# Attention, routed experts and a bilinear layer in one kernel: one branch for the general path, other banks for the seven products, gate weights padded to 128 columns

## The chip, the core and the metric

The kernel runs on one core of a Trainium2 chip. The core has TensorE (PE) for matmuls, with a loader for weights (PEld), VectorE (DVE), ScalarE (ACT), GpSimd (POOL) and a sync engine (SP) that issues most transfers. Each engine takes its own instructions in order, and they wait for each other through semaphores. Matmuls write into PSUM, which the kernel divides into eight banks of 128 x 512 words. The metric is device microseconds of one execution; lower is better.

## What is computed

The reference has three steps, one after the other, all in float32:

```python
# windowed attention: B, H, S, D = 4, 8, 576, 64; window 128, a bias by distance
attn = softmax(where(mask, scale * q @ k.T + bias, -1e9)) @ v
x = attn.transpose(0, 2, 1, 3).reshape(2304, 512)
# routed experts: 8 of them, 512 -> 1024 -> 512; each token goes to its best one
logits = x @ w_gate + modality_bias[modality_id]
x = gate_w[:, None] * (relu(x @ w1[e]) @ w2[e])      # e = argmax(logits)
# bilinear layer: 512 -> 1024, a product, 1024 -> 1024, 1024 -> 512
out = ((x @ m_w1) * (x @ m_w2)) @ m_w3 @ m_wout
```

## The kernel before

Nearly every product is made of three matmuls: each factor is split into a high part (an ACT copy, names ending in h) and the rest (a DVE subtraction, names ending in l), by `split` (lines 249 and 251), and high x high, high x low and low x high are summed (`mm3`, lines 266 to 268). The work goes through four stages.

*Attention* (about 0 to 264 us) runs over 40 units (a chunk of tokens and four heads; here a chunk has 128 tokens, or 64 at the end of a sequence): scores `S`, softmax, transposes of the probabilities, and `av`, the product with v, which has 64 columns. When a tile of 128 tokens is done, `gate_logits` (line 465) transposes it (`xtp`) and makes the logits `lg` in four products with the gate weights `wg`, which have 8 columns, one per expert (line 478). The trace shows each of these products as two rows. There are 18 such tiles in five groups, and after each group `route` finds the experts and ranks. In the same stage PE makes the product of `m_w3` and `m_wout` (`pw`, `w_step`), by a list of steps written out by hand (`W_STEPS`).

*The bridge* (264 to 303) makes the table of blocks and gathers the tokens; the rest of `pw` is done under it.

*The experts* (303 to 540) take five static blocks of 480 tokens (`NB_STATIC`), with tiles `ph` and `py`. Another number of blocks can be needed for other tokens; that is the general path, below. Under this stage DVE and ACT make sums of `m_w1` and `m_w2` for the next one.

*The bilinear layer* (540 to 818) goes over three groups g of 768 tokens. Each has eight steps f (`ab_step`, line 1183) and six tiles j (`out_step`, line 1234). A step f makes two products of 2 x 2 blocks with seven block products instead of eight: seven times six matmuls of 128 x 384 (line 1196), summed in four banks `x`, `y`, `z`, `v` with the tags S, V, P and G. S and P have two banks each, V and G one. The first halves of `x` and `v` are read (a copy `c1` by ACT, sums `c22`, `c12`, `c21` by DVE, line 1205) and then a second product is added into the same bank. The weights of a step are loaded (`load_wt`) and split (`split_wt`: two `wth` on ACT, two `wtl` on DVE) one step ahead, and the sums of the next group's x (`x2_sum`, seven splits `x2h`/`x2l`) come behind the first tile j. A tile j makes `po` in 24 matmuls of 128 x 512 with `ab` (split by `ab_split` in halves `abh`, `abl`) and `Whl`, the split product of W3 and Wout; its banks have the tag A, two of them. ACT scales it (`o`, line 1245) and POOL scatters it (line 1246). The `wh` splits of that product are made in the eight steps of group 0.

*The general path* stands at the end (lines 1312 to 1335), behind `If`s on the number of blocks `nb`. `rest(b)` is called for each static block and for the next one, and the bilinear layer comes a second time. With the inputs here `nb` is 5, and none of the seven `If`s is taken; each engine jumps over each part (lines 1315 and 1333).

What sets the order on an engine is the order of the program, unless a scheduler finds an instruction ready earlier: it follows the order in which the program is written, with priorities (`tc.high_priority`), and `tc.issue_after(x)` keeps what stands in it behind x on its engine. A tile of a pool with a tag waits until the tile that had its buffer is released.

Of the kernel before, what the change touches and what calls it, by code (L numbers as in the profile page):

```python
# [33 lines left out]
EARLY = 2  # L34
W_STEPS = [0, 0, 0, 0, 0, 0, 0, 0, 0, 0, 1, 1, 1, 2, 1, 2, 1, 1, 1, 2, 0, 1, 0, 2, 1, 1, 1, 0, 0, 3, 2, 1, 0, 1, 1, 0, 0, 2, 1, 1, 1, 2, 2, 1, 3, 0]
# [8 lines left out]
def kernel(  # L44
# [67 lines left out]
    wg = const.tile([P, ND, E], F32, tag="wg", name="wg")  # L112
# [94 lines left out]
    def build_constants2():  # L207
# [3 lines left out]
        nc.sync.dma_start(out=wg, in_=w_gate.rearrange("(c p) e -> p c e", p=P))  # L211
# [479 lines left out]
    def w3_transposes(i):  # L691
        x = st_w.pop(("x", i))
        h = w_p.tile([P, 4, P], F32R, tag="w3h", name=f"w3h_{i}", bufs=3)
        l = w_p.tile([P, 4, P], F32R, tag="w3l", name=f"w3l_{i}", bufs=3)
        tp = pst("A", [P, 4, P], f"w3tp_{i}")
        for j in range(4):
            nc.tensor.transpose(tp[:, j, :], x[:, j * P : (j + 1) * P], ident)
        split(h, l, tp)
        st_w["T", i] = (h, l)
# [6 lines left out]
    def w_step(k):  # L706
# [8 lines left out]
        if g == NG - 1:  # L715
            last["ev", fc] = nc.scalar.copy(wraw[:, fc, :], pw)
# [73 lines left out]

    def chunk_done(b, c):
# [5 lines left out]
        if j == groups[g][1] - 1:  # L797
            todo.append(lambda: route(g, *groups[g]))
# [232 lines left out]
    def run_blocks(b0, b1, extra, after=None):  # L1031
        g0, g1 = b0 * NS, b1 * NS
        for g in range(g0, min(g0 + SA, g1)):
            if after is None:
                split_w(g)
            else:
                with tc.issue_after(after):
                    split_w(g)
# [23 lines left out]
    for n in range(k_in, n_w):  # L1062
# [7 lines left out]
        w_step(n)  # L1070
    wstk.close()
# [91 lines left out]
    def split_wt(g, f):  # L1163
        w = wt[g, f] = []
        for k in range(2):
            h, l = (
                f_p.tile([P, 7, P], F32R, tag=f"w{x}", name=f"wt{x}_{g}_{f}_{k}", bufs=4)
                for x in "hl"
            )
            split(h, l, wt.pop(("raw", g, f, k)))  # L1170
            w.append((h, l))

    def bilinear(first):
# [9 lines left out]
        def ab_step(g, f):  # L1183
# [4 lines left out]
                for tag, n in (("S", 2), ("V", 1), ("P", 2), ("G", 1))  # L1188
# [15 lines left out]
            def add(out, in0, in1, op=ALU.add):  # L1204
                nc.vector.tensor_tensor(out=out, in0=in0, in1=in1, op=op)  # L1205
# [3 lines left out]
            c1, u, c22, c12, c21 = tmp("c1"), tmp("u"), tmp("c22"), tmp("c12"), tmp("c21")  # L1209
            prod(x, A11, B11, True)  # L1210
# [6 lines left out]
            add(c22, z, c22)  # L1217
            prod(x, A12, B21, False)
# [3 lines left out]
            prod(v, A22, T4, False)  # L1222
            add(c21, v, u)
            add(ab[g][:, f, TS:], c21, c22, ALU.mult)

        def ab_split(g, j, i):
# [4 lines left out]
            split(ah, al, ab[g][:, i * NMC // 2 : (i + 1) * NMC // 2, cs])  # L1231
            ab[g, j, i] = (ah, al)
# [21 lines left out]
        g2 = {}  # L1254
        if not first:
# [4 lines left out]
            split_wt(0, 0)  # L1260
            load_wt(0, 1)
        for g in range(NG2):
# [36 lines left out]
    jobs.setdefault(g_end - 1, []).append(lambda: split_wt(0, 0))  # L1299
    jobs.setdefault(g_end - 1, []).append(lambda: load_wt(0, 1))  # L1300
    jobs.setdefault(g_end - 1, []).append(load_nb)
    run_blocks(0, NB_STATIC, jobs, last["ev", NMC - 2].ins)
# [9 lines left out]
    def rest(b):  # L1312
        if b == NB_MAX:
            return
        with tc.If(nb > (b if b > NB_STATIC else NB_STATIC)):
            first_loads(b, b + 1)
            run_blocks(b, b + 1, {})
            if b + 1 > NB_STATIC:
                rest(b + 1)

    with tc.tile_pool(name="xr", bufs=2) as x_p, tc.tile_pool(name="fr", bufs=2) as f2_p:

        def h_tiles(b, m):
            return tuple(
                f2_p.tile([P, BLK], F32R, tag=f"h{x}", name=f"h{x}r_{b}_{m}", bufs=HB) for x in "hl"
            )
# [8 lines left out]
    x2stk.close()  # L1335
# [38 lines left out]
```

## Time and profile before

| | |
|---|---|
| median of 3 runs | 851.11 us (849.89 to 856.74) |
| the profiled execution | 848.0 us, of which the span of the trace is 846.3 |
| mean granted clock of PE | 0.943 of full speed |
| PE busy | 791.3 us (93%) in 4405 instructions |
| weight loads | 693.3 us (82%) |
| DVE, ACT, POOL busy | 519.8 (61%), 352.1 (42%), 73.7 (9%) |

The span is what the trace covers; 1.7 us of the profiled execution lie around it. A busy share near 100% means that PE always had a matmul under way, not that it streamed at its peak. [...]

### The profile page before, as it was taken

The page shows a single profiled execution, that of the slowest core. Times are in us where ns is not written, and L with a number is a line of the kernel's source. Part 1 is how long each engine was busy: PE and PEld are TensorE (multiplying, and loading weights), DVE is VectorE, ACT ScalarE, POOL GpSimd, SP SyncE. Part 2 cuts the span into 40 slices and gives each one's busy share as a digit, 9 for nine tenths or more (in the row PEclk, how much of TensorE's full clock was granted, in tenths as well). Part 3 has the DMA queues.
Part 4 walks back from the last instruction along what each step waited for, and adds up shares of the span by engine and source line. Part 5 has one row for each costly group of instructions (what it writes and reads, how often), then busy time and mean ns, then how long its engine had stood idle before and what let it go on. Part 6 is the DMA issues. An engine that isn't in the chain of part 4 may idle for free. (4 is left out here: it accounts for less than half of the span.)

```text
span 846.3 us, 12536 instructions
## 1 busy us (share of the span) xinstructions
PE 791.3 (93%) x4405; PEld 693.3 (82%) x4405; DVE 519.8 (61%) x1273; ACT 352.1 (42%) x755; POOL 73.7 (9%) x102
## 2 busy tenths in 40 slices
PE   8999999999999899999999999998999979999960
PEld 6897878898997678887888889997889968899750
DVE  4758596657567539796885644768446693476310
ACT  5846465765752423333345534334323252322220
POOL 4000200110102312020010000000100001100110
PEclk9959889999979999999999999997999989999985
DMA  8985464345212846969587425424223421240010
GB/s 153 366 241 142 113 169 124 63 117 125 77 38 77 221 141 204 311 187 329 168 287 236 167 67 182 151 95 131 100 81 100 127 92 38 81 131 3 25 57 9
DMA packets 126443, 116.88 MB, mean 138 GB/s; under 512 B 69597, under 2 KB 100701, under 8 KB 126350
## 3 DMA queue, kind: packets, MB, share of 16 engines
q1 hardware_dynamic: 119853, 101.16, 41.4%
q0 software_dynamic: 3616, 9.66, 3.6%
q10 hardware_dynamic: 2880, 4.92, 1.6%
q8 instruction: 47, 0.77, 0.4%
q14 instruction: 47, 0.38, 0.2%
HBM read 87.85 MB, written 27.68 MB: 137 GB/s over the span
## 5 line engine op out<-in xcount | busy, mean ns | idle before, releaser
L383 ACT ACTIVATE p<-p,mn 128x256 f32<-128x256 f32 (+2 forms) x144 | 67.8, 473 | 26.6 <-DVE mn L378 26.4
L251 DVE TENSOR_TENSOR fwl<-fw,fwh 128x1024 fp32r<-128x1024 f32 x40 | 48.7, 1223 | 48.4 <-ACT fwh L249 44.4
L249 ACT ACTIVATE fwh<-fw 128x1024 fp32r<-128x1024 f32 x40 | 42.1, 1060 | 73.9 <-PE ph L267 57.9
L266 PE MATMUL ph<-xbh,fwh 128*128 128x480 f32 x160 | 61.9, 388 | 3.1 <-DVE Whl L956 2.4
L249 ACT ACTIVATE wth<-wt 128x896 fp32r<-128x896 f32 x48 | 43.8, 948 | 48.9 <-PE pP L1196 32.7
L426 PE MATMUL av<-vr,pT 128*128 128x64 f32 x448 | 63.1, 286 | 0.0
L426 PEld LDWEIGHTS av<-vr,pT 128*128 128x128 f32 x448 | 60.9, 208 | 1.7 <-DVE w_wo L652 0.2
L267 PE MATMUL ph<-xbl,fwh 128*128 128x480 f32 x160 | 61.6, 385 | 0.0
L378 DVE CUSTOM_DVE_ANT_0 p<-S,bias 128x256 f32<-128x256 f32 (+1 forms) x128 | 43.4, 386 | 29.5 <-PE S L352 29.3
L267 PE MATMUL py<-Whl,fwh 128*128 128x480 f32 x160 | 61.2, 383 | 0.0
L268 PE MATMUL ph<-xbh,fwl 128*128 128x480 f32 x160 | 61.2, 382 | 0.0
L266 PE MATMUL po<-Whl,abh 128*128 128x512 f32 x144 | 58.2, 404 | 1.9 <-ACT abh L249 1.9
L251 DVE TENSOR_TENSOR wtl<-wt,wth 128x896 fp32r<-128x896 f32 x48 | 52.0, 1083 | 12.1 <-ACT wth L249 9.2
L268 PE MATMUL py<-Whl,fwl 128*128 128x480 f32 x160 | 59.1, 380 | 0.0
L267 PE MATMUL po<-Whl,abh 128*128 128x512 f32 x144 | 57.9, 402 | 0.0
L266 PE MATMUL py<-Whl,fwh 128*128 128x480 f32 x160 | 56.9, 380 | 0.0
L268 PE MATMUL po<-Whl,abl 128*128 128x512 f32 x144 | 56.4, 395 | 0.0
L251 DVE TENSOR_TENSOR abl<-ab,abh 128x512 fp32r<-128x512 f32 x36 | 24.6, 689 | 48.9 <-ACT abh L249 48.9
L249 ACT ACTIVATE abh<-ab 128x512 fp32r<-128x512 f32 x36 | 22.4, 630 | 67.3 <-PE po L267 56.0
L1205 DVE TENSOR_TENSOR c<-pG,u 128x384 f32<-128x384 f32 x48 | 26.6, 554 | 37.7 <-PE pG L1196 37.3
L404 PE MATMUL PT<-ident,p 128*128 128x128 f32 x224 | 42.9, 310 | 0.0
L1246 POOL DMA_INDIRECT out_dram<-o,sid x18 | 17.8, 990 | 283.0 <-ACT o L1245 278.7
(236 smaller groups left out, 2010.8 us busy)
## 6 DMA issues: line engine op xcount, KB each, us to landing
wt<-wT SPq DMA_DIRECT2D x48, 448.0 KB
fw<-in_moe_w_dram SPq DMA_DIRECT2D x40, 512.0 KB
raw_w<-in_moe_w_dram SPq DMA_DIRECT2D x16, 512.0 KB
raw_m<-in_moe_w_dram SPq DMA_DIRECT2D x32, 256.0 KB
wT<-ms SPq DMA_DIRECT2D x16, 448.0 KB
yT<-zf SPq DMA_DIRECT2D x20, 256.0 KB
yT<-y ACTq DMA_DIRECT2D x20, 240.0 KB
x<-yT SPq DMA_DIRECT2D x12, 384.0 KB
```

The costliest lines, as they stand in the source:

```text
L249: last["a"] = nc.scalar.activation(out=hi, in_=src, func=AF.Copy, scale=scale)
L251: last["v"] = nc.vector.tensor_tensor(out=lo, in0=src, in1=f32(hi), op=ALU.subtract)
L266: nc.tensor.matmul(dst, lhsT=lh, rhs=rh, start=start, stop=False)
L267: nc.tensor.matmul(dst, lhsT=lh, rhs=rl, start=False, stop=False)
L268: return nc.tensor.matmul(dst, lhsT=ll, rhs=rh, start=False, stop=stop)
L378: nc.vector.tensor_tensor_reduce(out=p[:, j, t, :nk], in0=s[j][:, t, :nk], in1=bi, scale=1.0, scalar=BIG, op0=ALU.add, op1=ALU.min, accum_ ...
L383: nc.scalar.activation(out=p[:, j, t, :nk], in_=p[:, j, t, :nk], func=AF.Exp, scale=-1.0, bias=m1, accum_out=sm[:, col : col + 1],)
L404: nc.tensor.transpose(pt[:, t, kb, :], p[:, j, t, kb * P : (kb + 1) * P], ident)
L426: nc.tensor.matmul(av[:, h, :], lhsT=pT[:, j, t, kb, :], rhs=raw["v", b, cc][:, h, :], start=(i == 0), stop=(i == len(kbs) - 1),)
L1205: nc.vector.tensor_tensor(out=out, in0=in0, in1=in1, op=op)
L1246: sc = nc.gpsimd.indirect_dma_start(out=out, out_offset=bass.IndirectOffsetOnAxis(ap=sid[g][:, j, 0:1], axis=0), in_=o, in_offset=None, bo ...
```

## The change

There are three edits, and some moves that go with them.

*One branch.* The seven `If`s become one, `If(nb > NB_STATIC)`. In it all blocks are computed again from the first, with the further blocks nested inside, and then the bilinear layer. What isn't taken is one part instead of seven.

*Padded gate weights.* `wg` has 128 columns per block of 128 rows instead of 8. POOL fills it with zeros, and the transfer writes the first 8. The logits' products are 128 columns wide, and DVE reads 8 of them.

*Two banks for each product.* In `ab_step`, `y` goes to V and G in turn, by the parity of f, and `v` goes to A, which has two banks that it shares with `po`.

The moves: `route` gets a high priority; the splits of the next weights, of `wh` and of the first `ab` are issued at fixed places in a step, behind the latest DVE sum; the next group's x is loaded in step 2 instead of 7, and its seven sums are spread over the six tiles j; the experts' first weight splits are issued behind the last split of `m_w3` instead of behind a copy of the product.

In the order of PE before, at the end of group 0, these rows stand where the bank `pG` of step 7 goes over from its first product to its second (a name ends in group, step, block of rows and a running number).

```order
L1196 MATMUL pG_0_7_6280<-x2h_0_5477,wth_0_7_1_6191 128x384
L1196 MATMUL pG_0_7_6280<-x2l_0_5478,wth_0_7_1_6191 128x384
L1196 MATMUL pG_0_7_6280<-x2h_0_5477,wtl_0_7_1_6192 128x384
L1196 MATMUL pG_0_7_6280<-x2h_0_5477,wth_0_7_0_6187 128x384
L1196 MATMUL pG_0_7_6280<-x2l_0_5478,wth_0_7_0_6187 128x384
```

The third row is the last of the first product, and the fourth begins the second one in the same bank, which DVE must have read in between. In the order of the changed kernel the first products end with these rows, the next tile's `po` among them.

```order
L1200 MATMUL pA_0_7_6277<-x2h_0_5478,wtl_0_7_1_6239 128x384
L1200 MATMUL pP_0_7_6276<-x2h_0_5478,wtl_0_7_1_6239 128x384
L268 MATMUL po_0_0_6343<-Whl_3596,abh_0_0_0_6242 128x512
L269 MATMUL po_0_0_6343<-Whl_3596,abh_0_0_0_6242 128x512
```

The second products then begin behind the twelfth `po` row, which is the first one here.

```order
L270 MATMUL po_0_0_6343<-Whl_3596,abl_0_0_0_6243 128x512
L1200 MATMUL pS_0_7_6274<-x2h_0_5478,wth_0_7_0_6206 128x384
L1200 MATMUL pS_0_7_6274<-x2l_0_5479,wth_0_7_0_6206 128x384
L1200 MATMUL pS_0_7_6274<-x2h_0_5478,wtl_0_7_0_6207 128x384
L1200 MATMUL pS_0_7_6274<-x2h_0_5478,wth_0_7_1_6238 128x384
L1200 MATMUL pS_0_7_6274<-x2l_0_5479,wth_0_7_1_6238 128x384
L1200 MATMUL pS_0_7_6274<-x2h_0_5478,wtl_0_7_1_6239 128x384
L1200 MATMUL pA_0_7_6277<-x2h_0_5478,wth_0_7_0_6206 128x384
```

The bank is `pA` now. The first row above ends its first product, and the last row begins its second; `pP`, twelve `po` rows and six `pS` rows stand between them.

In ACT's order before, the end of group 0 reads so: the last copy `c1`, the weights of group 1's steps 0 and 1, three of the sums of x, and the second half of `ab`.

```order
L1211 COPY c1_0_7_6281<-pS_0_7_6277 128x384
L249 ACTIVATE wth_1_0_0_6260<-wt_1_0_0_6195 128x896
L249 ACTIVATE wth_1_0_1_6264<-wt_1_0_1_6197 128x896
L249 ACTIVATE wth_1_1_0_6590<-wt_1_1_0_6268 128x896
L249 ACTIVATE wth_1_1_1_6594<-wt_1_1_1_6270 128x896
L249 ACTIVATE x2h_1_6380<-x2_1_6272 128x768 x3
L249 ACTIVATE abh_0_0_1_6343<-ab_0_5764 128x512
L249 ACTIVATE abh_0_1_0_6359<-ab_0_5764 128x512
```

In the changed kernel the same place reads so.

```order
L1224 COPY c1_0_7_6278<-pS_0_7_6274 128x384
L251 ACTIVATE wth_1_1_0_6605<-wt_1_1_0_6270 128x896
L251 ACTIVATE wth_1_1_1_6637<-wt_1_1_1_6272 128x896
L251 ACTIVATE x2h_1_6381<-x2_1_5900 128x768 x3
L251 ACTIVATE abh_0_0_1_6344<-ab_0_5757 128x512
L251 ACTIVATE abh_0_1_0_6360<-ab_0_5757 128x512
L251 ACTIVATE abh_0_1_1_6388<-ab_0_5757 128x512
L1261 ACTIVATE o_0_0_6376<-po_0_0_6343,g2_0_5747 128x512
L251 ACTIVATE abh_0_2_0_6404<-ab_0_5757 128x512
```

The two `wth` of step 0 have gone ahead of `c1`; the two of step 1, the three `x2h` and the `abh` stand behind it as they did, and the scaling of the first tile comes three rows after that `abh`.

On POOL, before, the constants of the beginning stand in this order, between the last memset of a padded q and the first selects of the mask.

```order
L202 MEMSET qz11_106 128x512
L204 IOTA ie_154 128x8
L734 IOTA ti_403 128x5
L180 AFFINE_SELECT scr_120<-scr_120 128x256
L734 IOTA ti_406 128x12
```

In the changed kernel the memset of `wg` stands among them.

```order
L203 MEMSET qz11_106 128x512
L205 IOTA ie_154 128x8
L212 MEMSET wg_75 128x512
L181 AFFINE_SELECT scr_120<-scr_120 128x256
L737 IOTA ti_404 128x5
```

It has come ahead of an AFFINE_SELECT of the attention's mask, and is 128 x 512.

The end of group 1 reads like that of group 0 in both kernels, with other names. The diff, without the loops and signatures around it:

```diff
+PRIO = 400
-    wg = const.tile([P, ND, E], F32, tag="wg", name="wg")
+    wg = a_p.tile([P, ND, P], F32, tag="wg", name="wg", bufs=1)
...
-        nc.sync.dma_start(out=wg, in_=w_gate.rearrange("(c p) e -> p c e", p=P))
+        nc.gpsimd.memset(wg, 0.0)
+        nc.sync.dma_start(out=wg[:, :, :E], in_=w_gate.rearrange("(c p) e -> p c e", p=P))
...
-        lp = pst("A", [P, E], f"lg_{i}")
+        lp = pst("A", [P, P], f"lg_{i}")
...
-        nc.vector.tensor_tensor(out=lg[g][:, pos, :], in0=lp, in1=bmod[:, i, :], op=ALU.add)
+        nc.vector.tensor_tensor(out=lg[g][:, pos, :], in0=lp[:, :E], in1=bmod[:, i, :], op=ALU.add)
...
+    def route_first(g):
+        with tc.high_priority(PRIO):
+            route(g, *groups[g])
...
-            todo.append(lambda: route(g, *groups[g]))
+            todo.append(lambda: route_first(g))
...
-    def split_wt(g, f):
-        w = wt[g, f] = []
-        for k in range(2):
...
+    def split_wt(g, f, k):
...
-        def ab_step(g, f):
+        def ab_step(g, f, before, between, after):
...
-                for tag, n in (("S", 2), ("V", 1), ("P", 2), ("G", 1))
+                for tag, n in (("S", 2), ("VG"[f % 2], 1), ("P", 2), ("A", 2))
...
+            behind(before)
             prod(x, A11, B11, True)
...
             prod(z, S1, T1, True)
             add(c22, z, c22)
+            behind(between)
             prod(x, A12, B21, False)
...
             prod(v, A22, T4, False)
+            behind(after)
             add(c21, v, u)
             add(ab[g][:, f, TS:], c21, c22, ALU.mult)
...
-                if n + 1 < NG2 * NMC:
-                    split_wt(*divmod(n + 1, NMC))
...
-                if f == NMC - 1 and g + 1 < NG2:
+                if f == 2 and g + 1 < NG2:
                     x2_load(g + 1)
-                ab_step(g, f)
+                before, between, after = None, None, None
+                if n + 1 < NG2 * NMC:
+                    nxt = divmod(n + 1, NMC)
+                    before = lambda: split_wt(*nxt, 0)
+                    between = lambda: split_wt(*nxt, 1)
                 if g == 0 and first:
-                    split(wh[:, f, :], wl[:, f, :], wraw[:, f, :])
-            ab_split(g, 0, 0)
+                    after = lambda: split(wh[:, f, :], wl[:, f, :], wraw[:, f, :])
+                if f == NMC - 2:
+                    between_ = between
+
+                    def between():
+                        between_()
+                        ab_split(g, 0, 0)
+
+                ab_step(g, f, before, between, after)
             for j in range(NTG):
                 out_step(g, j)
-                if j == 0 and g + 1 < NG2:
-                    for i in range(7):
-                        x2_sum(g + 1, i)
+                if g + 1 < NG2:
+                    for i in ([0, 1], [2], [3], [4], [5], [6])[j]:
+                        with tc.issue_after(last["s"].ins):
+                            x2_sum(g + 1, i)
...
-        with tc.If(nb > (b if b > NB_STATIC else NB_STATIC)):
...
-        for b in range(NB_STATIC):
-            rest(b)
-        rest(NB_STATIC)
-    x2_open()
-    with tc.tile_pool(name="cr", bufs=2) as c_p:
-        with tc.If(nb > NB_STATIC):
+    with tc.If(nb > NB_STATIC):
...
+            first_loads(0, NB_STATIC + 1)
+            run_blocks(0, NB_STATIC + 1, {})
+            rest(NB_STATIC + 1)
+        x2_open()
+        with tc.tile_pool(name="cr", bufs=2) as c_p:
             bilinear(False)
```

## Rows read from the trace of the kernel before

**Rows 1.** Busy time by stage; the first line names the columns.

```profile
core 0: us, PE busy (x) PEld busy (x) DVE busy (x) ACT busy (x) POOL busy (x), PEclk, DMA share, GB/s
20.00:264.00 244.00, 240.70 (x1743) 208.82 (x1742) 160.22 (x597) 144.80 (x435) 17.07 (x16) 0.90 0.52 141
600.00:680.00 80.00, 79.77 (x416) 74.10 (x415) 43.12 (x70) 24.11 (x34) 5.07 (x6) 1.00 0.32 105
```

**Rows 2.** Timeline of the span's end, POOL: start, length, instruction.

```profile
819.29 0.97 POOL L1246 DMA_INDIRECT out_dram<-o,sid  x1 [4.33 <-ACTq L1315]
```

**Rows 3.** The closing jumps and drains by line: count, ns min/median/max, first and last start.

```profile
L1315 PEldq COMPARE_BRANCH  x6: 352/4030/4751, 814.6 to 835.7; - x6
...
L1333 PEldq COMPARE_BRANCH  x1: 4592/4592/4592, 840.5 to 840.5; - x1
...
L1369 POOLq DRAIN  x3: 46/107/4635, 832.1 to 845.9; - x3
```

**Rows 4.** Busy time in stretches at half clock, and at full (150 to 199.5).

```profile
45.90:66.40 20.50, 20.50 (x98) 19.28 (x97) 11.17 (x36) 8.89 (x26) 0.00 (x0) 0.50 0.81 217
83.40:90.30 6.90, 6.90 (x26) 5.63 (x27) 4.25 (x16) 3.13 (x11) 0.00 (x0) 0.51 0.69 183
107.30:114.20 6.90, 6.90 (x25) 5.74 (x26) 6.90 (x23) 5.22 (x17) 0.00 (x0) 0.51 0.81 171
199.50:202.90 3.40, 3.40 (x11) 2.81 (x12) 1.43 (x6) 0.52 (x2) 0.00 (x0) 0.50 0.00 0
233.60:243.90 10.30, 10.30 (x51) 9.29 (x50) 5.61 (x23) 5.78 (x19) 0.00 (x0) 0.50 0.07 25
...
150.00:199.50 49.50, 48.78 (x410) 43.09 (x409) 32.29 (x138) 34.26 (x108) 5.14 (x5) 1.00 0.42 100
...
581.80:592.00 10.20, 8.02 (x22) 6.48 (x21) 9.44 (x13) 6.29 (x9) 0.00 (x0) 0.50 0.38 117
...
687.60:694.40 6.80, 6.21 (x17) 5.36 (x18) 6.77 (x10) 3.56 (x6) 0.00 (x0) 0.50 0.39 124
```

**Rows 5.** Of line 478 alone: the stretches ahead of four falls; columns PE, PEld.

```profile
41.00:45.90 4.90, 1.06 (x8) 0.97 (x8) 1.00 0.95 292
79.00:83.40 4.40, 0.00 (x0) 0.00 (x0) 1.00 0.33 115
...
195.00:199.50 4.50, 0.96 (x8) 0.96 (x8) 1.00 0.78 231
229.00:233.60 4.60, 1.06 (x8) 0.97 (x8) 1.00 0.24 76
```

**Rows 6.** Timeline, PE: logits and transposes; length covers the whole row of them.

```profile
32.77 0.97 PEld L478 LDWEIGHTS lg<-wg,xT 128*128 128x128 f32 x8
32.77 1.06 PE L478 MATMUL lg<-wg,xT 128*128 128x8 f32 x8
...
33.69 0.64 PE L284 MATMUL ktp<-ident,kr 128*128 128x128 f32 x4
```

**Rows 7.** Timeline of PE at the second group's end; idle in brackets.

```profile
682.38 0.45 PE L1196 MATMUL pG<-x2h,wth 128*128 128x384 f32 x1 [1.93 <-DVE c L1205]
...
686.70 0.44 PE L1196 MATMUL pS<-x2h,wth 128*128 128x384 f32 x1 [1.97 <-ACT x2h L249]
688.19 0.69 PE L1196 MATMUL pS<-x2h,wth 128*128 128x384 f32 x1 [1.04 <-DVE ab L1205]
688.85 0.80 PE L266 MATMUL po<-Whl,abh 128*128 128x512 f32 x1
```

**Rows 8.** Timeline of ACT at the second group's end.

```profile
684.12 1.79 ACT L249 ACTIVATE wth<-wt 128x896 fp32r<-128x896 f32 x2 [4.66 <-issue]
...
688.17 1.15 ACT L249 ACTIVATE abh<-ab 128x512 fp32r<-128x512 f32 x2
```

**Rows 9.** A memset on POOL by line, and a split on DVE from the page.

```profile
L202 POOL MEMSET qz<- x4: 514/514/515, 2.2 to 4.0; 128x512 f32 x4
...
L251 DVE TENSOR_TENSOR abl<-ab,abh 128x512 fp32r<-128x512 f32 x36 | 24.6, 689 | 48.9 <-ACT abh L249 48.9
```

More of the change, by code (lines that the diff above doesn't have):

```diff
@@ L698, in w3_transposes @@
         split(h, l, tp)
+        st_w["last"] = (last["a"], last["v"])
         st_w["T", i] = (h, l)
@@ L715, in w_step @@
         if g == NG - 1:
-            last["ev", fc] = nc.scalar.copy(wraw[:, fc, :], pw)
+            nc.scalar.copy(wraw[:, fc, :], pw)
     units = [(b, c, hq) for b in range(B) for c in range(NF + 1) for hq in range(NQ)]
@@ L1029, in first_loads, with run_blocks @@
         gather_x(b0)
-    def run_blocks(b0, b1, extra, after=None):
+    def run_blocks(b0, b1, extra, after=()):
         g0, g1 = b0 * NS, b1 * NS
         for g in range(g0, min(g0 + SA, g1)):
-            if after is None:
+            with ExitStack() as st:
+                for a in after:
+                    st.enter_context(tc.issue_after(a.ins))
                 split_w(g)
-            else:
-                with tc.issue_after(after):
-                    split_w(g)
         for u in range(NU):
@@ L1070 @@
         w_step(n)
+    w3_last = st_w["last"]
     wstk.close()
@@ L1161, in load_wt @@
             wt["raw", g, f, k] = t
-    def split_wt(g, f):
-        w = wt[g, f] = []
-        for k in range(2):
[L1166 to L1171, printed above, removed]
+    def split_wt(g, f, k):
+        h, l = (
+            f_p.tile([P, 7, P], F32R, tag=f"w{x}", name=f"wt{x}_{g}_{f}_{k}", bufs=4) for x in "hl"
+        )
+        split(h, l, wt.pop(("raw", g, f, k)))
+        wt.setdefault((g, f), []).append((h, l))
     def bilinear(first):
@@ L1204, in add, with behind @@
             def add(out, in0, in1, op=ALU.add):
-                nc.vector.tensor_tensor(out=out, in0=in0, in1=in1, op=op)
+                last["d"] = nc.vector.tensor_tensor(out=out, in0=in0, in1=in1, op=op)
+            def behind(job):
+                if job is None:
+                    return
+                with ExitStack() as st:
+                    if "d" in last:
+                        st.enter_context(tc.issue_after(last["d"].ins))
+                    job()
             if f == 0:
@@ L1231, in ab_split @@
             split(ah, al, ab[g][:, i * NMC // 2 : (i + 1) * NMC // 2, cs])
+            last["s"] = last["v"]
             ab[g, j, i] = (ah, al)
@@ L1254, in bilinear @@
         g2 = {}
+        last.pop("d", None)
         if not first:
@@ L1259, in bilinear @@
             load_wt(0, 0)
-            split_wt(0, 0)
+            for k in range(2):
+                split_wt(0, 0, k)
             load_wt(0, 1)
@@ L1298 @@
     jobs.setdefault(g_end - 3, []).append(lambda: load_wt(0, 0))
-    jobs.setdefault(g_end - 1, []).append(lambda: split_wt(0, 0))
+    jobs.setdefault(g_end - 1, []).append(lambda: [split_wt(0, 0, k) for k in range(2)])
     jobs.setdefault(g_end - 1, []).append(lambda: load_wt(0, 1))
     jobs.setdefault(g_end - 1, []).append(load_nb)
-    run_blocks(0, NB_STATIC, jobs, last["ev", NMC - 2].ins)
+    run_blocks(0, NB_STATIC, jobs, w3_last)
     xstk.close()
@@ L1312, in rest, with h_tiles @@
     def rest(b):
-        if b == NB_MAX:
-            return
-        with tc.If(nb > (b if b > NB_STATIC else NB_STATIC)):
-            first_loads(b, b + 1)
-            run_blocks(b, b + 1, {})
-            if b + 1 > NB_STATIC:
-                rest(b + 1)
[L1321 to L1326, printed above, removed]
-        for b in range(NB_STATIC):
-            rest(b)
-        rest(NB_STATIC)
-    x2_open()
-    with tc.tile_pool(name="cr", bufs=2) as c_p:
-        with tc.If(nb > NB_STATIC):
+        if b < NB_MAX:
+            with tc.If(nb > b):
+                first_loads(b, b + 1)
+                run_blocks(b, b + 1, {})
+                rest(b + 1)
+    with tc.If(nb > NB_STATIC):
+        with tc.tile_pool(name="xr", bufs=2) as x_p, tc.tile_pool(name="fr", bufs=2) as f2_p:
+            def h_tiles(b, m):
+                return tuple(
+                    f2_p.tile([P, BLK], F32R, tag=f"h{x}", name=f"h{x}r_{b}_{m}", bufs=HB)
+                    for x in "hl"
+                )
+            first_loads(0, NB_STATIC + 1)
[3 more added lines that the diff above has]
+        with tc.tile_pool(name="cr", bufs=2) as c_p:
             bilinear(False)
-    x2stk.close()
+        x2stk.close()
 _INS = [
```

## The prediction

> **What bounds the kernel now.** I read the page first, then the busy time by stage, then the end of the span, then the stretches at the low clock, then the waits of TensorE (PE) at the three places where a group of the bilinear stage ends. The reader is to see that PE is the bound nearly everywhere: it is busy 240.70 of 244 us in attention and 79.77 of 80 in the run of a bilinear group [rows 1]. So an edit pays only where it takes away PE's own waits, raises PE's clock, or shortens what lies behind the last matmul.
>
> Three such places are in reach of this change. **The end:** the last result leaves on POOL at 819.29 and takes 0.97 us [rows 2], yet the span is 846.3 us long. PE then walks through seven compare-and-branch instructions, one for each `If` that isn't taken. The first is short (0.35 us), and the others take up to 4.75 us; the last starts at 840.5 and takes 4.59 [rows 3], so it ends at 845.1. Nothing else is left by then but the program's closing, 1.2 us. **The clock in attention:** the granted clock falls to half (1.2 GHz) five times, for 48 us in all [rows 4]. **The group ends:** there PE stands with nothing to stream [rows 7].
>
> **The change part by part.**
>
> *One branch instead of seven.* Six jumps go. The one that stays is taken by PE while its last matmuls still run, as the first is now. What is late next is POOL, whose last scatter ends at 820.26 (819.29 + 0.97), then its drain, which took 4.64 us at the longest [rows 3], then the closing of 1.2: 820.3 + 4.6 + 1.2 = 826.1, so 846.3 - 826.1 = 20.2 us are gained. If the drain takes nothing, the end is 821.5 and the gain 24.8; if a jump of 4.75 stands in front of the drain, the end is 830.9 and the gain 15.4. I take 20, since POOL does drain and its own jumps are no bound now.
>
> *Padded logits.* Each of the 18 tiles has four products `lg`, which the trace shows as eight matmul rows of 8 columns: 144 in all. They become 128 columns wide. Eight with 8 columns take 1.06 us from first start to last end; four transposes with 128 columns take 0.64 [rows 6]. With one row's length (0.26 and 0.31 us) taken off, that is a pitch of 0.114 and 0.110 us. The pitch is set by something other than the columns: loading the weights of the eight takes 0.97 us as well. So the padding costs nothing in pitch, and only each tile's last product ends some 0.05 us later, at most 18 x 0.05 = 0.9 us. The upper bound is 144 x 0.05 = 7 us, if every row grew by the difference in length. I take 0, since the nearest row is the transposes' of the same shape.
>
> [...]
>
> What the padding can give lies in the clock. In the stretches right before it fell at 45.9, 199.5 and 233.6, eight of the narrow `lg` rows stood [rows 5]: PE was occupied but streamed few columns. At half clock 98, 11 and 51 matmuls were done in 20.5, 3.4 and 10.3 us [rows 4], 160 in 34.2 us. At full clock the stage does 410 in 49.5 us, 8.3 per us; 160 would take 19.3, so these three stretches cost 14.9 us. Wide rows give the array 16 times the columns there. The other two falls (83.4 and 107.3) have 6.9 us each and 51 matmuls, a loss of 13.8 - 6.1 = 7.7; one has no `lg` ahead of it and the other comes after a stall, so I leave them. The instructions of attention stand in a slightly different order, so some other thin stretch may fall instead: I take 12 of the 14.9. The bounds are 0 (every fall comes back elsewhere) and 22.6 (none is left).
>
> *Two banks for each product.* They pay only where PE waits for a bank. In the run of a group it doesn't: 600 to 680 us has 0.2 us of idle time [rows 1]. At the second group's end it waits 1.93 us for VectorE (DVE) to read bank `pG`, then 1.97 for ScalarE (ACT) to split the next group's x, then 1.04 for a bank of `pS`, and the first `po` starts at 688.85 [rows 7]. The new order puts twelve `po` matmuls between the two uses of the bank (`pA` now), which is about 2.8 us of cover, so the 1.93 goes. What follows stays: ACT's queue ahead of the second half of `po` is the same list in both (two `wth`, three `x2h`, then `abh`), from 684.12 to the middle of the row of two at 688.17 [rows 8], and it starts only when the last products have read the weights. PE ends its products at 684.73 (686.70 less the 1.97) and gets `po` 4.1 us later; in the changed order it has two matmuls in between, so it idles about 3.8 us where it idled 4.9. That is 1.1 us. The first group's end goes the same way, and the last one, with no next group behind it, has little to gain. Sum: about 2 us. The clock falls there today, for 10.2 and 6.8 us, and an idle stretch of 4 us in one piece won't spare that; I count no gain. Bounds: -8 (both falls go as well) to +4 (the new order queues `pA` and `po` on the same two banks `A`, and some 0.3 to 0.6 us of new waits at each end, plus a longer fall).
>
> *The rest.* The 128 x 512 MEMSET of `wg` stands on POOL ahead of the selects that DVE's bias waits for; one of that shape takes 0.51 us [rows 9]. With no cover at the start, +0.5. The routing's priority, the later `wh` splits, the earlier x2 load and the issue orders move instructions under PE's stream: PE's own order from the end of attention to the start of the bilinear stage is the same row for row, so that stretch keeps its time. Without that cover the eight `wh` splits, of 0.69 us each by a split of the same shape [rows 9], would cost 5.5; DVE has the room, with 43 of 80 us busy in the run of a group [rows 1].
>
> **Sum.** 848.0 (the profiled execution: span 846.3, 1.7 around it) - 20 - 12 - 2 + 0.5 = 814.5. The median of the runs, 851.11, lies 3.1 above the profiled one, so I add 3.1: 817.6, about 818.
>
> **Rivals.**
> *The clock falls anyway.* The falls follow thin stretches, and the stretches with 64-column `av` products are thin too; one fall today has no `lg` before it. Then attention gains nothing: 818 + 12 = 830.
> *All falls go.* Attention gains 22.6 and the group ends 8: 818 - 10.6 - 6 = 801. Against it: the idle stretch at the group ends stays.
> *The end isn't about the jumps.* If the seven are cheap and PE waits there for something that one branch needs too, as the moving of semaphores of the part not run, the end stays: 848.0 - 12 - 2 + 0.5 + 3.1 = 837.6. Against it: PE's jumps follow each other back to back when all others are through [rows 3].
> [...]
> *Slower.* The clock doesn't come back after a group's end, because the new order there mixes matmuls with waits. At half clock these stretches lost about half their time (6.8 us with 17 matmuls [rows 4], against 416 in 80 us, 5.2 per us: 3.5). To eat the forecast gain of 33 us it would need some 65 us more at half clock, of the 160 us that the two later groups run; from there on it decides, and with 82 us the time would be 860. Today the clock comes back after 6.8 to 10.2 us.
>
> **How the numbers follow.** The forecast has 0.5 (810 to 826). The clock falling anyway 0.25 (826 to 836), all falls gone 0.13 (798 to 810), the end unchanged 0.06 (836 to 842), slower or no gain 0.06. The range of 803 to 836 leaves out half of the third, and the last two: 0.19. Within 1% of 851.11, about what a measurement of this kernel can tell from no change, is 842.6 to 859.6. Faster holds the first four less a part at the edge, 0.93; same 0.04; slower 0.03.
>
> **What will show it.** The end: one compare-and-branch per engine, and at most 9 us between the last matmul's end and the span's. The padding: 144 `lg` rows of 128 columns at a pitch near 0.11 us, and no fall of the clock right after a stretch with `lg`; attention (first `lg` to last) shorter by some 12 us. The group ends: no wait before the second half of `pA`, and one of about 4 us split by two `pS`. I am wrong on the clock if the 1.2 GHz time before 264 us is above 30 us, on the banks if PE waits inside a group, and on the end if POOL's drain is followed by something that isn't in the trace of before.

## The result, and the profile after

The changed kernel takes 805.0 us (median of 4 executions, 802.9 to 808.9), and the kernel before 850.5 in the same comparison (4 executions, 844.5 to 856.7). The ratio is 0.947, with a 95% interval from 0.939 to 0.955. The profiled execution took 805.8 us, with a span of 804.0, which is 42.3 us shorter than the span of before. The kernel before spread by up to 37 us from one execution to another on one chip (834.9 to 871.6, at mean granted clocks of 0.958 and 0.912); so I compare medians of all executions, with their ranges.

Three stretches cover nearly all of the span. This is the busy time by stretch in the changed kernel: attention from 20 us to the end of the last `lg`, two pieces of it at the low clock, the bilinear layer from the first product to the last `po`, and what lies behind. The first line names the columns.

```profile
core 0: us, PE busy (x) PEld busy (x) DVE busy (x) ACT busy (x) POOL busy (x), PEclk, DMA share, GB/s
20.00:244.30 224.30, 221.50 (x1739) 191.96 (x1738) 157.50 (x600) 145.16 (x437) 16.95 (x16) 0.98 0.58 152
30.20:33.60 3.40, 3.40 (x20) 3.40 (x17) 3.40 (x14) 2.56 (x9) 0.00 (x0) 0.50 1.06 398
238.40:241.80 3.40, 3.40 (x17) 3.17 (x18) 0.86 (x2) 0.00 (x0) 0.55 (x1) 0.50 0.18 39
498.00:792.70 294.70, 285.97 (x1449) 260.47 (x1447) 181.13 (x279) 95.19 (x141) 18.23 (x18) 0.98 0.30 95
792.70:804.00 11.30, 0.01 (x1) 0.00 (x0) 0.00 (x0) 0.69 (x1) 0.97 (x1) 0.59 0.08 28
```

The same three stretches of the kernel before:

```profile
20.00:262.80 242.80, 239.50 (x1738) 207.84 (x1737) 159.03 (x594) 144.80 (x435) 17.07 (x16) 0.90 0.52 140
516.80:818.30 301.50, 289.36 (x1449) 264.43 (x1447) 175.39 (x273) 97.81 (x141) 17.04 (x18) 0.97 0.29 93
818.30:846.30 28.00, 0.00 (x0) 0.00 (x0) 0.00 (x0) 0.69 (x1) 0.97 (x1) 0.54 0.08 19
```

The last `lg` ends 18.5 us earlier (244.3 against 262.8), the bilinear layer takes 294.7 us instead of 301.5, and the end takes 11.3 instead of 28.0: 18.5 + 6.8 + 16.7 = 42.0 of the 42.3. What lies between them, the bridge and the experts, starts and ends earlier by the same amount. The clock is the mark of the first gain: 0.98 instead of 0.90. The five falls of [rows 4] in attention, 48 us, have become two of 3.4 us. What the prediction and the expectations call 1.2 GHz is the granted clock of 0.50 in these rows.

The logits' rows have 128 columns, and eight of them take 1.16 us where eight of 8 columns took 1.06 [rows 6]. This is TensorE's timeline, with start, length and instruction:

```profile
35.72 1.16 PE L480 MATMUL lg<-wg,xT 128*128 128x128 f32 x8
```

At the second group's end TensorE no longer waits between the two products of a bank, as it did for 1.93 us [rows 7]. What is left are two waits. TensorE's timeline, the idle time before an instruction in brackets:

```profile
659.77 0.34 PE L1200 MATMUL pP<-x2h,wtl 128*128 128x384 f32 x1
662.01 0.65 PE L1200 MATMUL pS<-x2h,wth 128*128 128x384 f32 x2 [1.90 <-ACT x2h L251]
664.00 0.50 PE L268 MATMUL po<-Whl,abh 128*128 128x512 f32 x1 [1.33 <-ACT abh L251]
```

ACT's timeline shows why, with the same list as in [rows 8]: the weights, three `x2h`, and only then the second half of `ab`.

```profile
659.44 1.79 ACT L251 ACTIVATE wth<-wt 128x896 fp32r<-128x896 f32 x2 [4.49 <-PE pP L1200]
661.13 2.29 ACT L251 ACTIVATE x2h<-x 128x768 fp32r<-128x768 f32 x3
663.33 1.14 ACT L251 ACTIVATE abh<-ab 128x512 fp32r<-128x512 f32 x2
```

The end has one jump for each engine. These are the jumps, the semaphore instruction of POOL's queue and the drains, by line, with count, ns (min, median, max) and the first and last start:

```profile
L1347 PEldq COMPARE_BRANCH  x1: 3913/3913/3913, 789.0 to 789.0; - x1
...
L1347 POOLq COMPARE_BRANCH  x1: 53/53/53, 794.1 to 794.1; - x1
L1347 POOLq INC_SWDGE_SEM  x1: 1308/1308/1308, 797.2 to 797.2; - x1
...
L1396 POOLq DRAIN  x3: 46/106/4635, 798.6 to 803.8; - x3
```

The last scatter stands on POOL's timeline here:

```profile
793.71 0.97 POOL L1262 DMA_INDIRECT out_dram<-o,sid  x1 [4.34 <-ACT o L1261]
```

PE's jump lies under its last matmuls now: 3.91 us from 789.0, against 792.7 for the last matmul's end. But POOL isn't through when its scatter ends at 794.7. The trace of before has the same semaphore instruction behind six of its branches:

```profile
L1315 POOLq INC_SWDGE_SEM  x6: 1284/1284/1303, 820.0 to 828.9; - x6
```

### The profile page after: what moved, and what is told of

Its sections match the earlier page's. It is cut to its first block, busy times and chain, and to the rows that moved or that the text cites. A ratio compares the mean times of both kernels' runs of the same rounds, so it can differ in the third digit from the quotient of the medians.

```text
span 804.0 us, 12404 instructions
## 1 busy us (share of the span) xinstructions
PE 768.8 (96%) x4405; PEld 673.2 (84%) x4405; DVE 519.6 (65%) x1273; ACT 349.5 (43%) x755; POOL 73.9 (9%) x103
## 4 chain that ended last, share of the span: by engine, by line
PE 64%; issue 23%; DMA 4%; DVE 3%; ACT 3%; POOL 2%; SPq 1%; ACTq 0%; POOLq 0%; DVEq 0%
PE av L428 6%; PE S L354 5%; PE ph L268 4%; PE ph L269 4%; PE ph L270 4%; PE py L269 3%; PE py L268 3%; PE py L270 3%; PE PT L406 3%; PE lg L480 2%; PE pS L1200 2%; PE pP L1200 2%; PE pA L1200 2%; PE pw L268 2%; PE pw L270 2%
## 5 line engine op out<-in xcount | busy, mean ns | idle before, releaser
L268 PE MATMUL po<-Whl,abh 128*128 128x512 f32 x144 | 59.5, 413 | 4.6 <-ACT abh L251 4.6
L428 PE MATMUL av<-vr,pT 128*128 128x64 f32 x448 | 59.6, 275 | 0.1
L269 PE MATMUL po<-Whl,abh 128*128 128x512 f32 x144 | 58.8, 408 | 0.0
L428 PEld LDWEIGHTS av<-vr,pT 128*128 128x128 f32 x448 | 57.1, 197 | 1.9 <-ACT pT L407 0.3
L1209 DVE TENSOR_TENSOR c<-pA,u 128x384 f32<-128x384 f32 x48 | 26.8, 558 | 34.4 <-PE pA L1200 32.1
L406 PE MATMUL PT<-ident,p 128*128 128x128 f32 x224 | 39.7, 288 | 0.1
```

What stands on the lines that cost most here:

```text
L268: nc.tensor.matmul(dst, lhsT=lh, rhs=rh, start=start, stop=False)
L269: nc.tensor.matmul(dst, lhsT=lh, rhs=rl, start=False, stop=False)
L406: nc.tensor.transpose(pt[:, t, kb, :], p[:, j, t, kb * P : (kb + 1) * P], ident)
L428: nc.tensor.matmul(av[:, h, :], lhsT=pT[:, j, t, kb, :], rhs=raw["v", b, cc][:, h, :], start=(i == 0), stop=(i == len(kbs) - 1),)
L1209: last["d"] = nc.vector.tensor_tensor(out=out, in0=in0, in1=in1, op=op)
```

## The experiments

Each kernel was executed four or six times beside the kernel before. Before had a median of 851.75 us (835.1 to 857.7) beside one branch alone, padded logits alone, 8 columns again and the bilinear layer alone, all on one chip; on a second chip it had 846.6 (838.9 to 859.6) beside 32 columns, the two experiments on banks and the one without the general path, and 849.4 (834.9 to 871.6) beside the two with columns read several times over, the tiles in halves and the changed kernel again. The windows are those of the first table, placed by each kernel's own last `lg`, first product and last `po`.

**One branch alone.** The end of the kernel before, from `nb = regs["nb"]` on, is replaced by that of the changed kernel:

```diff
-        for b in range(NB_STATIC):
-            rest(b)
-        rest(NB_STATIC)
...
+    with tc.If(nb > NB_STATIC):
...
+            first_loads(0, NB_STATIC + 1)
...
```

> The kernel before with the general path in one branch, nothing else. Theory A (the three edits give separate gains): from PE's last matmul to the span's end 11.3 us as in the changed kernel, against 28.0 before, so 16.7 us less: about 834 us against 850.5. Attention and the bilinear stage keep their times (last lg near 263 us, group to group 101.8 us). Rival (the end is short only because the last matmuls end otherwise, or one branch over everything takes as long as seven): 845 to 851 us.

```profile
20.00:247.60 227.60, 225.51 (x1739) 195.69 (x1738) 158.96 (x596) 144.27 (x437) 17.07 (x16) 0.96 0.56 151
500.60:804.10 303.50, 290.80 (x1449) 265.77 (x1447) 175.56 (x273) 97.68 (x141) 17.50 (x18) 0.97 0.29 93
804.10:815.50 11.40, 0.03 (x1) 0.00 (x0) 0.00 (x0) 0.69 (x1) 0.97 (x1) 0.62 0.08 27
```

The median is 833.3 us (817.3 to 840.2), 18.4 less than before, and the end takes 11.4 us instead of 28.0. So the end's gain is 16.6 us, and it belongs to this edit. The first row holds a surprise: attention is 15 us shorter than in the profile of before, at a clock of 0.96 instead of 0.90, although every engine has the same instructions in the same order up to the first branch. In these two executions the program alone didn't fix the falls. So theory A holds for the end, while attention didn't keep its time (the last `lg` ends at 247.6, not near 263).

**Padded logits alone.** The edits of `wg` and `lp` are made in the kernel before.

```diff
-    wg = const.tile([P, ND, E], F32, tag="wg", name="wg")
+    wg = a_p.tile([P, ND, P], F32, tag="wg", name="wg", bufs=1)
...
+        nc.gpsimd.memset(wg, 0.0)
...
-        lp = pst("A", [P, E], f"lg_{i}")
+        lp = pst("A", [P, P], f"lg_{i}")
```

> The kernel before with the gate weights padded to 128 columns, nothing else; routing without priority. Theory A (the wide logits hold the clock): time at 1.2 GHz before the bridge falls from 48 us to 10 or less, the last lg ends near 245 instead of 263 us, about 832 us against 850.5. Rival (the order of instructions that came with the routing's priority holds the clock): three or more falls stay, last lg near 260, 846 to 851 us.

```profile
20.00:240.70 220.70, 218.38 (x1738) 188.53 (x1737) 156.47 (x596) 144.82 (x437) 16.97 (x16) 1.00 0.58 154
496.80:796.30 299.50, 285.89 (x1449) 262.19 (x1447) 175.35 (x273) 97.33 (x141) 17.65 (x18) 0.98 0.30 94
```

The median is 826.0 us (824.7 to 831.3), 25.8 less than before, and its range doesn't touch that of before. Attention ran at full clock from 20 us to the end. The priority of the routing isn't needed for it; what that priority does by itself wasn't run.

**The changed kernel with 8 columns again.** The same edits are undone.

```diff
...
-        lp = pst("A", [P, P], f"lg_{i}")
+        lp = pst("A", [P, E], f"lg_{i}")
...
```

> The changed kernel with the gate weights at 8 columns again. Theory A: the falls of the clock in attention come back, 30 to 50 us at 1.2 GHz before the bridge, and 15 to 19 us are lost: 820 to 824 us. Rival (routing's priority and the order do it): 805 to 808 us, at most 10 us at 1.2 GHz there.

```profile
20.00:270.80 250.80, 247.78 (x1737) 215.87 (x1736) 158.30 (x596) 145.72 (x436) 16.05 (x16) 0.87 0.52 137
```

The median is 829.2 us (819.7 to 835.3), some 22 to 24 more than the changed kernel (805.0 here, 807.3 when it ran again). Theory A is right that the falls come back, but its 820 to 824 put the price too low.

**32 columns.**

```diff
-    wg = a_p.tile([P, ND, P], F32, tag="wg", name="wg", bufs=1)
+    wg = a_p.tile([P, ND, 32], F32, tag="wg", name="wg", bufs=1)
...
-        lp = pst("A", [P, P], f"lg_{i}")
+        lp = pst("A", [P, 32], f"lg_{i}")
```

> The changed kernel with the gate weights padded to 32 columns instead of 128. The pitch of the logits stays near 0.12 us. Theory A (how many columns the logits stream decides): some falls of the clock in attention come back, 15 to 35 us at 1.2 GHz before the bridge, 811 to 822 us, and a wide spread between executions as with 8 columns. Rival (any padding is enough, by the zeros or the other order): 803 to 809 us, within 10 us at 1.2 GHz.

```profile
20.00:249.70 229.70, 225.65 (x1742) 194.98 (x1740) 159.04 (x597) 144.25 (x436) 16.81 (x16) 0.97 0.59 150
```

```profile
43.73 1.03 PE L480 MATMUL lg<-wg,xT 128*128 128x32 f32 x8
```

The second fence is TensorE's timeline of one tile's logits. The median is 810.5 us (808.0 to 812.0), far from the 829.2 of 8 columns. Neither expectation holds in full: the time lies between the two ranges, the profile has some 14 us at half clock in attention (a mean of 0.97 over 229.7 us), and the spread is narrow.

**8 columns in memory, 128 in the stream.** The weights stay at 8 columns, and each matmul reads them 16 times over. There are no zeros, no memset and no larger tile of weights.

```diff
-                lp, lhsT=xT[:, d, :], rhs=wg[:, d, :], start=(d == 0), stop=(d == ND - 1)
+                lp, lhsT=xT[:, d, :], rhs=wg[:, d : d + 1, :].to_broadcast([P, 16, E]), start=(d == 0), stop=(d == ND - 1)
...
```

> The changed kernel with the gate weights at 8 columns in memory, read 16 times over by each matmul, so that it streams 128 columns without padding, zeros or a memset. Theory A (the columns that the logits stream hold the clock): like the changed kernel, within 4 us of it (801 to 809), 17 us or less at 1.2 GHz before the bridge. Rival (the zeros in the array, or the memset and the new place in memory, do it): like the kernel with 8 columns, 819 to 835 us.

```profile
20.00:247.40 227.40, 224.79 (x1747) 194.50 (x1745) 158.62 (x597) 144.50 (x436) 17.19 (x16) 0.98 0.57 151
```

The median is 810.2 us (804.6 to 813.1), beside 807.3 for the changed kernel on the same chip, and far from the 829.2 of 8 columns. That is 2.9 us from the changed kernel, as theory A allows, though just above its 801 to 809. So the clock of 0.98 in attention, where 8 columns had 0.87, came with the columns that the logits stream; the zeros and the memset aren't needed. But 810.2 is also what 32 columns gave: the medians set 8 columns apart from the rest, and don't tell 32 from 128.

**256 columns in the same way.**

> The same with 256 columns. Theory A: of the 3 to 14 us at 1.2 GHz that are left in attention some go, but a matmul of 256 columns sets a pitch of its own: a row of S with 256 columns goes at 0.12 us, as the logits do, so no cost; 800 to 806 us. Rival (the array's time is now used up): 144 rows by some 0.05 us, 7 us more than with 128 columns.

```profile
20.00:257.90 237.90, 235.98 (x1739) 202.08 (x1738) 158.40 (x597) 144.74 (x437) 16.30 (x16) 0.99 0.53 143
```

```profile
44.44 1.95 PE L479 MATMUL lg<-wg,xT 128*128 128x256 f32 x8
```

The median is 818.7 us (816.1 to 824.0), 8.5 above the 128 columns. Theory A fails, and the rival's 7 us is near. The clock is at 0.99, but the eight rows of a tile take 1.95 us instead of 1.16, which is 18 x 0.8 = 14 us for all; attention is 237.9 - 227.4 = 10.5 longer. My comparison with the rows of S was wrong. In the code their factors are of the type fp32r and the logits' are f32; that this makes the difference wasn't run.

**The bilinear layer alone.** Everything from `split_wt` to the end of `bilinear` is that of the changed kernel, in the kernel before.

> The kernel before with the changed bilinear stage alone: two banks for each product, splits at fixed places, x loaded early and its sums spread. Theory A: the two periods from one group's end to the next shrink from 101.8 to 98.0 us, falls of the clock at the two ends 3.4 us each instead of 10.2 and 6.8; 843.5 us against 850.5. Rival (the shorter falls came from the earlier stages): 849 to 852 us.

```profile
20.00:264.60 244.60, 241.15 (x1738) 208.04 (x1737) 159.27 (x596) 145.16 (x437) 17.06 (x16) 0.90 0.52 139
515.80:813.50 297.70, 288.98 (x1449) 263.23 (x1447) 181.18 (x279) 95.20 (x142) 18.22 (x18) 0.97 0.29 94
```

The median is 843.3 us (836.1 to 843.7), 8.5 less than before, and the ranges overlap. The layer takes 297.7 us at the same mean clock (0.97) as the 301.5 of before. PE's idle time in it is 297.7 - 289.0 = 8.7 us, against 301.5 - 289.4 = 12.1. So 3.8 us of the 8.5 lie in the layer, nearly all of them idle time. Theory A named the time, but not for its reason: the falls at the first two ends are 6.8 us each here, not 3.4, and there is one of 3.4 at the third.

**The old banks in the new order.**

```diff
-                for tag, n in (("S", 2), ("VG"[f % 2], 1), ("P", 2), ("A", 2))
+                for tag, n in (("S", 2), ("V", 1), ("P", 2), ("G", 1))
```

> The changed kernel with the banks of before in the seven products (V and G, one bank each), and the changed order of issue. At a group's end only six matmuls, about 1.1 us, then stand between the two uses of bank G. Theory A (the banks give the gain of the bilinear stage, through the cover at the group ends): about 1 us more of waits at each of the three ends and longer falls of the clock, so the stage takes 298 to 301 us instead of 294.7; 809 to 811 us. Rival (the order of issue gives it): 804 to 807 us.

```profile
502.80:794.60 291.80, 283.43 (x1449) 260.71 (x1447) 181.35 (x279) 95.63 (x141) 16.95 (x18) 0.99 0.30 96
```

```profile
664.06 0.66 PE L1200 MATMUL pS<-x2h,wth 128*128 128x384 f32 x2 [1.90 <-ACT x2h L251]
666.05 0.50 PE L268 MATMUL po<-Whl,abh 128*128 128x512 f32 x1 [1.33 <-ACT abh L251]
```

The second fence is TensorE's timeline at the second group's end. The median is 801.6 us (799.2 to 808.0): theory A fails, and the rival holds, with a time below its range. The waits are those of the changed kernel, 1.90 and 1.33, and the idle time in the layer is 291.8 - 283.4 = 8.4 us, not more than with the new banks. The order puts only six matmuls between the two uses of bank G here, and at this end TensorE's timeline shows no wait ahead of the second use, six `pG` rows from 659.87 us.

**The new banks in the old order.** The same line the other way round, in the kernel with padded logits alone.

> The kernel with padded gate weights alone (825.99 us, bilinear stage 299.5 us from its first product to the last tile), with the new banks added and nothing of the new order of issue. The order of TensorE at a group's end then has twelve po and six matmuls between the two uses of the bank, as in the changed kernel. Theory A (banks): 295 to 296 us for the stage, 821 to 823 us. Rival (order of issue): 299 to 300 us, 825 to 827.

```profile
496.10:794.00 297.90, 287.17 (x1449) 261.85 (x1447) 175.33 (x273) 97.46 (x142) 17.28 (x18) 0.98 0.29 94
```

TensorE's timeline at the second group's end, where the bank goes over to its second product:

```profile
659.13 0.45 PE L1197 MATMUL pA<-x2h,wth 128*128 128x384 f32 x1 [0.23 <-DVE c L1206]
```

The median is 824.5 us (818.9 to 825.3) beside 826.0 with the old banks, which is from another chip; the stage's 297.9 us lie between the two expectations. The wait at the bank is 0.23 us where it was 1.93. The idle time in the layer is 297.9 - 287.2 = 10.7 us, against 299.5 - 285.9 = 13.6. So the banks alone take away the wait that they were meant for, and bring nothing on top of the new order, which takes it away too.

**No general path.**

```diff
-    with tc.If(nb > NB_STATIC):
...
-            rest(NB_STATIC + 1)
-            bilinear(False)
```

> The changed kernel without the general path: the branch and all behind it are left out, so it holds for these inputs alone. It measures what the one branch that stays still costs. After the last scatter (0.97 us) the changed kernel shows POOL's jump until 796.8, semaphores and one INC_SWDGE_SEM of 1.31 us, a drain of 4.64 us and 0.8 us of closing. Theory A (POOL's jump, its semaphores and its drain are the tail): the jump's 2.1 us behind the scatter and the semaphores' 1.7 us go, the drain stays: from the last matmul to the end 7 to 8 us instead of 11.3, 801 to 802 us. Rival B (the drain belongs to the branch): 3 to 4 us, about 797. Rival C (the jump is hidden): 804 to 806.

```profile
800.70:808.10 7.40, 0.00 (x0) 0.00 (x0) 0.00 (x0) 0.69 (x1) 0.97 (x1) 0.66 0.09 35
```

```profile
L1370 POOLq DRAIN  x3: 46/108/5848, 801.4 to 807.8; - x3
```

The end takes 7.4 us instead of 11.3, as theory A had it. The second fence has POOL's drains by line: the long one lasts until 801.4 + 5.85 = 807.3, which is 4.6 us behind the scatter's end at 802.6. So the drain isn't the branch's. The median, 804.5 us (801.3 to 809.8), doesn't show the gain of 3.9 us, and lies where rival C had it; but the jump isn't hidden, since the end is 3.9 us shorter. The profiled execution, at 809.8 the longest, had a clock of 0.96 in attention and 0.97 in the layer: its last `lg` ends 4.3 us later than in the profile of the changed kernel (248.6 against 244.3), and its layer takes 296.9 us instead of 294.7.

**Two tiles in halves.** What the trace after shows as left, the waits of 1.90 and 1.33 us at the group ends, gets twelve `po` of the next tile as cover.

```diff
+        halves_ = [(0, 0), (1, 0), (0, 1), (1, 1)] + [(j, h) for j in range(2, NTG) for h in range(2)]
...
-            for j in range(NTG):
-                out_step(g, j)
-                if g + 1 < NG2:
+            for j, h in halves_:
+                out_step(g, j, h)
+                if g + 1 < NG2 and h == 1:
```

> The changed kernel with the first two tiles of each group made in halves: first half of tile 0, first half of tile 1, then the second halves. Twelve po matmuls of tile 1 (2.8 us) then stand behind the last products, where TensorE waits 1.91 and 1.33 us for the next x and for the second half of ab (1.90 at the last group). Theory A (these waits and the fall of the clock that follows them are what is left of the group ends): waits of 0.5 us or less, no fall at the three ends, the bilinear stage 286 to 289 us instead of 294.7, some 6 to 9 us less than the changed kernel. Rival (the work is only moved, and the wait comes back behind the halves or at the next step's first products): within 2 us of the changed kernel.

```profile
20.00:240.80 220.80, 218.71 (x1739) 188.99 (x1738) 156.14 (x596) 144.91 (x437) 16.39 (x16) 1.00 0.58 154
494.90:777.20 282.30, 280.48 (x1449) 256.88 (x1448) 180.50 (x279) 94.53 (x142) 19.48 (x18) 1.00 0.31 100
```

TensorE's timeline at the first group's end:

```profile
558.69 0.34 PE L1200 MATMUL pP<-x2h,wtl 128*128 128x384 f32 x1
558.87 0.43 PE L268 MATMUL po<-Whl,abh 128*128 128x512 f32 x1
...
561.70 0.52 PE L1200 MATMUL pS<-x2h,wth 128*128 128x384 f32 x2
562.94 0.50 PE L268 MATMUL po<-Whl,abh 128*128 128x512 f32 x1 [0.72 <-ACT abh L251]
```

The median is 793.0 us (790.3 to 798.3), 14.3 less than the changed kernel on the same chip, so this version beats both. Twelve `po` stand behind the last product at 558.69, and 0.72 us of wait is left, a little more than the 0.5 that I had allowed. The idle time in the layer is 282.3 - 280.5 = 1.8 us, and its clock doesn't fall in this execution.

**The changed kernel again**, beside the halves and the columns read several times over:

> The changed kernel again, beside the three others on one chip: 803 to 809 us, and attention's time at 1.2 GHz between 3 and 17 us from one execution to another.

```profile
20.00:243.30 223.30, 220.29 (x1738) 190.24 (x1737) 156.26 (x596) 144.80 (x437) 16.40 (x16) 0.98 0.58 154
495.60:790.10 294.50, 285.78 (x1449) 260.31 (x1447) 181.01 (x279) 95.16 (x141) 18.23 (x18) 0.98 0.30 95
```

The median is 807.3 us (803.1 to 808.6). Against it the halves save 294.5 - 282.3 = 12.2 us in the layer. Of these 6.9 are idle time (8.7 to 1.8), and 285.8 - 280.5 = 5.3 are matmuls that no longer run at half clock. I had expected 6 to 9 in all.

## Why the prediction was right, and where it wasn't

**In sum.** I forecast 818, and 805.0 was measured. That lies inside the range, near its lower end, and on the predicted side. But it is not the case to which I gave 0.5 (810 to 826); it is the one to which I gave 0.13, where nearly all falls go (798 to 810). The terms were 20, 12, 2 and -0.5; the traces show 16.7, 18.5 (the memset in it) and 6.8, 42.0 instead of 33.5. The size of the sum is in part luck: the end gave less than I said, and the other two more, some of it by how often the clock happened to fall in the two profiled executions. The +3.1 from profiled to median was chance of the executions: the profile after lies at 805.8 and its median at 805.0.

**The end: 16.7 instead of 20.** The gain comes from folding the branches, as I said, and the rival that the jumps are cheap is out: with one branch alone the end shrinks as much, by 16.6 us. The step that failed is "its own jumps are no bound now". POOL's jump starts at 794.1, and its next instructions come at 796.8. Then semaphores and the INC_SWDGE_SEM of 1.31 us run until 798.5, the drain (4.64) until 803.2, and the closing to 804.0. From the scatter's end at 794.7 to the drain 3.9 us pass that I had set at zero; without the general path just these 3.9 go. The INC_SWDGE_SEM of 1.3 us at each of POOL's branches stood in the trace of before and could have been read there. I had the drain's 4.64 right, and took the closing too long (1.2 against 0.8). The sign that I named, at most 9 us behind the last matmul, failed with 11.3.

**The clock in attention: 18.5 instead of 12.** I chose between bounds of 0 and 22.6 by giving each fall to what stood ahead of it, and left out two of the five, one without an `lg` there and one behind a stall. That step failed. With one branch alone, the same instructions had 0.96 where before had 0.90; so here a fall in one execution can't be given to the rows ahead of it. What can be told is the whole stage over several executions. The medians are 829.2 us with 8 columns, 810.5 with 32, and with 128 columns 805.0, 807.3 and, read 16 times over, 810.2. Attention's clock is 0.87 to 0.96 in four profiles with 8 columns, 0.97 with 32, and 0.96 to 1.00 in eight with 128. The price of the low clock was about right: with 48.0 - 6.8 = 41.2 us less of it 18.5 were saved, 0.45 per us; my 14.9 + 7.7 for 48.0 us were 0.47.

The rival in which the clock falls anyway didn't come as a time, but a fall among `av` products did. Near the end of attention stand 32 of them with 64 columns, from 234.7 to 239.1 us in the changed kernel, and there the clock falls at 238.4. In two of the eight profiles with 128 columns attention has a clock of 1.00, so the same rows pass at full clock; the other six have 0.96 to 0.98. These are the logits behind them, in TensorE's timelines of the changed kernel, where the clock had fallen, and of padded logits alone, where it hadn't:

```profile
239.06 2.07 PE L480 MATMUL lg<-wg,xT 128*128 128x128 f32 x8
236.81 1.16 PE L479 MATMUL lg<-wg,xT 128*128 128x128 f32 x8
```

**The padding's own cost.** I took 0 in pitch, and at most 0.9 for the last products. Eight rows take 1.16 us instead of 1.06, so 18 x 0.1 = 1.8 us if all of it is on the path.

**The group ends: 6.8 instead of 2.** The wait for `pG` went, and the waits for x and for `ab` stayed, 1.90 and 1.33 (3.2 us, where I had said about 3.8). The idle time of the layer fell by 12.1 - 8.7 = 3.4, and I had said 2. The other 3.4 are matmuls' busy time, 289.4 - 286.0, since the falls at the ends were 3.4 us each in this profile. I had counted no gain for the clock, and the runs don't show that the change gives one. The layer of the changed kernel has the same idle time of 8.7 us in the run without the general path and in the run with 32 columns, but busy times that lie 5.4 us apart, at 0.97 and at 0.99:

```profile
503.80:800.70 296.90, 288.15 (x1449) 262.33 (x1447) 181.18 (x279) 95.17 (x141) 18.23 (x18) 0.97 0.29 94
503.40:794.90 291.50, 282.77 (x1449) 258.08 (x1447) 181.17 (x279) 95.24 (x141) 18.23 (x18) 0.99 0.30 96
```

The step that failed is the one that gave the gain to the banks alone. In the old order they take the wait away, as I said; but with the old banks and the new order the idle time is the same as with the new ones (8.4 us), so the change's gain doesn't hang on them.

**What stays open.** Why the time at low clock at a group's end varies between 3.4 us and 10.2, with waits of 3.2 to 4.9 us there, wasn't settled, nor what decides where in attention the clock falls in a given execution. Which of the moves in the new order (the splits at fixed places, the earlier load of x, its sums spread over the tiles) takes the wait away wasn't tried one by one.

## What to carry to other kernels

Where TensorE's clock falls at changing places in a stage of narrow matmuls, as in attention here (0.87 to 0.96 in four profiles with 8 columns), compare several executions, not places in one trace, and try the narrow ones wider, as far as their pitch doesn't grow (eight rows took 1.16 us with 128 columns and 1.95 with 256); reading the same columns several times over does it without memory (810.2 us beside 807.3). Fold branches that aren't taken into one (16.6 us here), and then count what each engine still does behind its last work, POOL's jump, semaphores and drain above all (9.3 us here, from the last scatter's end to the span's). When a wait at a seam is removed, look at what is late next and put ready work of the next tile there: that was worth 14 us more here, nearly as much as the branch.

## What the hardware showed that I had not expected

The same instructions spread by 37 us between executions of the kernel before (834.9 to 871.6 in 11), and those of the changed kernel by 6 (803.1 to 808.6 in 6).

At full clock the eight f32 rows of a tile take 0.95 to 1.06 us with 8 columns, 1.00 to 1.08 with 32 (three tiles) and 1.06 to 1.16 with 128, but 1.95 to 2.00 with 256 (three tiles): from 8 to 128 the columns cost some 0.1 us a tile.

POOL's drain takes 4.64 us in the changed kernel, as in the kernel before, where its last scatter had ended 12 us ahead of it. Without a branch it ends the same 4.6 us behind the scatter. So it wasn't shorter where the scatter had long ended.

The one jump of the changed kernel took 3.91 us on PE, under its last matmuls. On POOL its row is 0.05 us long, but 2.7 us pass from it at 794.1 to POOL's next instruction at 796.8.
